# An index spread in two row tiles of TensorE, with the expert layer's issue order written anew

## The chip, the cores and the metric

The kernel runs on one core of one Trainium2 chip. The metric is the device time of one execution in microseconds (us). A core has five engines that work at the same time, each through its own list of instructions in order: TensorE (PE, matmuls; its weight loads are shown as PEld), VectorE (DVE), ScalarE (ACT), GpSimd (POOL) and SyncE (SP, which here issues the transfers). They wait for each other through semaphores. Matmul results land in PSUM, eight banks of 2 KB for each of 128 partitions, and have to be copied out by DVE or ACT.

## The reference

The input is 2048 tokens of 512 features. The first half is a state space convolution over the tokens (layer norm, an FFT convolution with a kernel made from 128 modes per feature, a skip). The second half is the expert layer, where the change lies:

```python
q1, q2 = q[..., :dk], q[..., dk:]          # q = layernorm(h) @ w_q, 32 heads
s1 = einsum("nhd,ed->nhe", q1, k1)         # 16 scores for each token and head
s2 = einsum("nhd,ed->nhe", q2, k2)         # 16 more
eidx = argmax(s1) * 16 + argmax(s2)        # K = 1: one of 256 experts
g = softmax over one score = 1
act = gelu(einsum("nd,nhd->nh", xf, u[eidx]))
out = einsum("nh,nhd->nd", act, v[eidx])   # sum over 32 heads
h2 = h + out
```

## The kernel before

The convolution is done as DFTs by matmul and takes most of the first 300 us. Behind it the expert layer goes through eight tiles of 256 tokens, b = 0 to 7. For each tile these steps run (the names are those of the tiles in the profile; a number behind a name is the tile b, or for mx, eq, kq, ks, ei and ix the half tile 2b + k of 128 tokens):

1. ib, h: the last step of the inverse transform on PE (L1036), with 32-column tiles of the array, and DVE's sum with the input xt (L1043).
2. hs, mean, hc, hhi, hlo: POOL adds four feature groups, PE sums over partitions, DVE subtracts the mean, ACT and DVE split the result into a high and a low part for exact products. vs, var, rstd do the same for the variance.
3. sc (L1150): scores for 960 columns, in four blocks per half tile, one for each quarter q of the features, each of which needs the weights w_hi and w_lo of that quarter. xu (L1157): products with all 256 rows of u; act: their gelu on ACT.
4. mx, eq, kq (DVE), ks (POOL), ei, ix (DVE): the place of the largest score, as a number from 0 to 255 for each token and head. ix is 128 tokens by 32 heads.
5. ixt, ixT: PE turns ix so that the 32 heads stand on 32 partitions (L1242), ACT copies it out (L1246).
6. bc, idxb: the index spread. For each g of 8, a matmul with the selection matrix sel_s[:, g] takes four heads and writes each on 32 partitions (L1258). Contraction is over the 32 partitions of ixT. Two matmuls of 256 tokens fill a PSUM bank, which ACT copies out as bf16 (L1262).
7. oh (L1280): DVE compares idxb with the expert codes, eight times per tile. cnt (L1290): PE counts the one-hots over the heads, with four 32-column tiles of the array. ta and actT bring act into the same layout; DVE multiplies.
8. whi, wlo, o, ob: the product with v in exact parts, the sum with h, and the store.

Tile 7 does steps 5 to 8 in two halves of 128 tokens, with all eight one-hots, counts and products for each half.

The code does not issue this in the order in which it is written. Each step is put in a list with `plan.add`, with its engine, what it reads and writes and which PSUM buffer it takes (`take="psD"`) or gives back. `plan.run(ORDER)` then issues the steps by a table of numbers. A number is the place of the step in the list of adds, so a step that is left out shifts all later numbers. An engine executes in that order and never passes a waiting instruction. The order also decides which buffers come next: psD has four buffers of a bank each, psC two of two banks for the scores. Transfers are all issued by SP, in order.

Before the expert layer the weights w_q0 to w_q3 are loaded, split by ACT (w_hi) and DVE (w_lo). They use the same buffers as later loads: w_q2 and w_q3 those of xt, and w_q0 and w_q1 those of sel_f (the selection matrix as loaded), u and v.

## Time and profile before

| | |
|---|---|
| time, median of 3 runs | 504.2 us (504.18 to 505.11) |
| profiled execution, its own time | 504.94 us |
| profiled execution, span from first to last instruction | 503.2 us |
| mean granted TensorE clock | 0.986 |
| PE busy | 449.0 us (89%) |
| DVE busy | 407.8 us (81%) |
| ACT, POOL busy | 298.3, 325.5 us |
| spread matmuls bc (L1258) | 56 of 256 columns, 16 of 128 |
| evictions idxb (L1262) | 32, 588 ns each, 17.5 us |

In rows of groups, the columns are: line, engine, operation, output<-input, partitions x elements, count | busy us, mean ns of one | idle time of the engine ahead of it and who ended that. The chain of waits has the start, the length and the piece. A timeline row has the start, the length, the engine, the line, the operation and, in brackets, the idle time ahead of it with its releaser. In the table of stretches each engine's busy us stands with its number of instructions, and then the clock, the share of DMA and GB/s. PE's busy time includes the pipelined tail of a matmul, so that of many short matmuls in a row is read from the starts or the chain, not from the mean.

### The profile page before, as it was taken

The numbers are of one execution on the slowest core, as the hardware profiler recorded it, in microseconds if no ns is written. First come the engines' busy times: TensorE is split into PE (matmuls) and PEld (weight loads), VectorE is DVE, ScalarE is ACT, GpSimd is POOL, SyncE is SP. The second block draws the span as 40 slices with busy tenths as digits, with TensorE's granted clock in tenths as the row PEclk, the third lists the DMA queues.
The fourth block names the chain that finished last, engine by engine and source line by source line (L and its number), as shares of the span: only waits on it lengthen the run. The fifth ranks groups of instructions, "written<-read, shape, count | busy, mean of one in ns | idle before, by whom it ended". The sixth has DMA issues, their size and how long they took to land.

```text
span 503.2 us, 16702 instructions
## 1 busy us (share of the span) xinstructions
PE 449.0 (89%) x7206; PEld 390.3 (78%) x7206; DVE 407.8 (81%) x708; ACT 298.3 (59%) x594; POOL 325.5 (65%) x344
## 2 busy tenths in 40 slices
PE   0266879999998999999998889999999999999985
PEld 0144568888997999889997787877878888787874
DVE  5998998899968998899745574888979686978984
ACT  4867799967987588967965362644043430416230
POOL 4989989999999999997824303572163516536130
PEclk9998799999999999999999899999999999999999
DMA  8959474234033300631017689310171311010012
GB/s 253 403 198 381 143 288 148 66 86 179 2 111 124 85 3 1 212 126 45 1 61 259 200 275 283 127 61 1 57 227 55 109 63 43 1 44 0 1 68 62
DMA packets 27362, 61.05 MB, mean 121 GB/s; under 512 B 7028, under 2 KB 14456, under 8 KB 26136
## 3 DMA queue, kind: packets, MB, share of 16 engines
q1 hardware_dynamic: 27136, 59.85, 34.9%
q8 instruction: 57, 0.93, 0.7%
q10 hardware_dynamic: 152, 0.13, 0.1%
q14 instruction: 17, 0.14, 0.1%
HBM read 46.08 MB, written 13.89 MB: 119 GB/s over the span
## 4 chain that ended last, share of the span: by engine, by line
PE 50%; DVE 22%; ACT 10%; POOL 10%; issue 4%; DMA 3%; SPq 1%; ACTq 0%; DVEq 0%; POOLq 0%
PE sc L1150 12%; PE ia L764 9%; DVE oh L1280 5%; PE s2yk L488 3%; PE xu L1157 3%; PE kps L690 3%; PE s2yu L488 3%; POOL pg L557 3%; PE s1u L471 3%; DVE st L232 2%; PE o L1327 2%; PE ib L1036 2%; PE cnt L1290 2%; ACT t L645 2%; POOL mg L594 2%
## 5 line engine op out<-in xcount | busy, mean ns | idle before, releaser
L557 POOL TENSOR_TENSOR pg<-PS 128x1024 int32<-128x1024 int32 x32 | 68.8, 2150 | 0.5
L588 POOL TENSOR_TENSOR mg<-TS 128x1024 f32<-128x1024 f32 x32 | 62.6, 1958 | 7.2 <-PE kps L690 4.5
L1280 DVE TENSOR_SCALAR oh<-idxb,ec_s 128x2048 bf16<-128x2048 bf16 (+1 forms) x72 | 50.3, 757 | 6.8 <-ACT idxb L1262 6.8
L764 PE MATMUL ia<-ca_s,U 128*128 128x128 f32 x256 | 50.6, 280 | 0.4 <-POOL U L743 0.4
L1060 POOL TENSOR_TENSOR vs<-hc 128x256 f32<-128x256 f32 x8 | 7.0, 872 | 62.6 <-ACT hc L1083 62.6
L1192 POOL TENSOR_TENSOR ks<-kq 128x512 f32<-128x512 bf16 x16 | 17.2, 1078 | 45.9 <-DVE kq L1186 44.8
L645 ACT ACTIVATE t<-t,halfpi 128x512 f32<-128x512 f32 x64 | 42.4, 662 | 2.1
L1150 PE MATMUL sc<-w_hi,hhi 128*128 128x480 f32 x128 | 42.4, 412 | 0.0
L644 ACT ACTIVATE t<-pg 128x512 f32<-128x512 int32 x64 | 38.9, 609 | 3.2 <-DVE gf L652 2.2
L764 PEld LDWEIGHTS ia<-ca_s,U 128*128 128x128 f32 x256 | 39.8, 196 | 0.6 <-POOL U L743 0.6
L647 ACT ACTIVATE t<-pg 128x512 f32<-128x512 int32 x64 | 38.2, 608 | 2.8 <-POOL pg L557 1.5
L764 PE MATMUL ia<-ca_s,yk 128*128 128x128 f32 x192 | 38.1, 280 | 0.4 <-DVE mg L664 0.4
L1150 PE MATMUL sc<-w_lo,hhi 128*128 128x480 f32 x128 | 38.4, 380 | 0.0
L1150 PE MATMUL sc<-w_hi,hlo 128*128 128x480 f32 x128 | 38.3, 380 | 0.0
L594 POOL TENSOR_TENSOR mg<-TS 128x512 f32<-128x512 f32 x32 | 37.4, 1170 | 0.4
L690 PE MATMUL kps<-mg 128*32 128x64 f32 x1024 | 34.0, 230 | 3.8 <-DVE mg L664 2.2
L488 PE MATMUL s2yk<-yk,c_s 128*128 128x128 f32 x256 | 34.7, 282 | 1.1 <-ACT yk L474 0.7
L471 PE MATMUL s1u<-c_s,xs 128*64 128x128 f32 x512 | 33.3, 277 | 2.5 <-DVE xs L508 1.6
L690 PE MATMUL kps<-gf 128*32 128x64 f32 x1024 | 33.7, 229 | 1.8 <-issue 1.8
L488 PEld LDWEIGHTS s2yk<-yk,c_s 128*128 128x128 f32 x256 | 30.6, 191 | 4.2 <-issue 1.4
L488 PE MATMUL s2yu<-yu,c_s 128*128 128x128 f32 x256 | 32.6, 279 | 0.3
L471 PEld LDWEIGHTS s1u<-c_s,xs 128*64 128x64 f32 x512 | 27.6, 137 | 5.4 <-DVE xs L508 1.7
(198 smaller groups left out, 1377.5 us busy)
## 6 DMA issues: line engine op xcount, KB each, us to landing
wq<-wq SPq DMA_DIRECT2D x25, 512.0 KB, 4.5
t_d<-T SPq DMA_DIRECT2D x24, 256.0 KB, 3.4
Tb<-t_d SPq DMA_DIRECT2D x8, 768.0 KB, 6.0
x<-xa SPq DMA_DIRECT2D x8, 512.0 KB, 5.6
xs<-xb SPq DMA_DIRECT2D x16, 256.0 KB, 5.3
xt<-xt SPq DMA_DIRECT2D x8, 512.0 KB, 4.8
out<-ob SPq DMA_DIRECT2D x7, 512.0 KB, 3.0
c_s<-wq SPq DMA_DIRECT2D x4, 512.0 KB, 8.3
```

The costliest lines, as they stand in the source:

```text
L471: T.matmul(ps[64 * k:64 * k + 64, g, :], lhs8(4 * n + g), c1_s[:, k], start=True, stop=True)
L488: T.matmul(ps[:, k, :], c2_s[:, kk, :], y[:, :, kk, :], start=True, stop=True)
L557: G.tensor_tensor(view(pg, 0, [[32, 2 * NC], [8, 4], [1, 8]]), view(t["PS"], 1024 + off, [[1, 2 * NC], [128, 4], [0, 8]]), view(t["PS"], 8 ...
L588: G.tensor_tensor(view(mg, 0, [[96, NC], [8, 8], [1, 8]]), view(ts, 512 + 8 * o, [[8, NC], [1, 8], [0, 8]]), view(ts, 8 * o, [[8, NC], [0, ...
L594: G.tensor_tensor(view(mg, 64, [[96, NC], [8, 4], [1, 8]]), view(ts, 1536 + o, [[1, NC], [64, 4], [0, 8]]), view(ts, 1024 + 8 * o, [[8, NC ...
L644: A.activation(p, pg[:, :, k], AF.Abs)
L645: A.activation(p, p, AF.Sin, scale=-SINSCALE, bias=halfpi)
L647: A.activation(p, pg[:, :, k], AF.Sin, scale=SINSCALE)
L690: T.matmul(kps[32 * q:32 * q + 32, 2 * g + h, :], m[:, d, 64:96], m[:, d, 0:64], start=(e == 0), stop=(e == 1))
L764: T.matmul(ps[:, g, :], t[:, 4 * n + g].rearrange("p a b -> p (a b)"), ca_s[:, s, :], start=(s == 0), stop=(s == 1))
L1150: T.matmul(ps[:, 512 * h:512 * h + 480], t[x_][:, q, ts], I[w_][:, q, 480 * h:480 * h + 480], start=(q == 0 and x_ == w_), stop=(q == 3 an ...
L1280: V.tensor_scalar(oh[:, :, 0:ln], t["idxb"][:, :, sl], S["ec"][:, 4 * e + j:4 * e + j + 1], None, op0=ALU.is_equal)
```

## The change

ix is written twice side by side, 64 columns instead of 32. The transpose then turns both copies at once, so that ixT has 64 partitions: heads 0 to 31 on partitions 0 to 31 and again on 32 to 63. The selection matrix is stored twice in the same way. The eight spread matmuls of a tile are issued in pairs: the first of a pair contracts over partitions 0 to 31, the second over 32 to 63, and the two write into two different PSUM buffers. One step of PE now takes two psD buffers and holds four matmuls (eight of 128 columns in tile 7); the evictions stay as they were, one for each buffer. There are 16 steps fewer in the list, 1712.

```diff
 def sel_load():
-    ...name="sel_f").rearrange("p a b -> p (a b)")[0:32].rearrange(
+    ...name="sel_f").rearrange("p a b -> p (a b)")[0:64].rearrange(
...
-        S["sel"] = I["wp"].tile([32, 8, 128], BF16, name="sel_s")
+        S["sel"] = I["wp"].tile([64, 8, 128], BF16, name="sel_s")
...
-            t[f"ix{k}"] = hp_("ix", n, [P, 32], BF16)
-            V.scalar_tensor_tensor(t[f"ix{k}"], ef[:, :, 0], 16.0, ef[:, :, 1], op0=ALU.mult, op1=ALU.add)
+            t[f"ix{k}"] = hp_("ix", n, [P, 64], BF16)
+            a, b_ = (ef[:, :, j].unsqueeze(1).to_broadcast([P, 2, 32]) for j in range(2))
+            V.scalar_tensor_tensor(t[f"ix{k}"].rearrange("p (c h) -> p c h", c=2), a, 16.0, b_, op0=ALU.mult, op1=ALU.add)
...
-                job["ps"] = tp = I["psD"].tile([32, 256], BF16, tag="m", name=f"ixt{b}_{lo}")
+                job["ps"] = tp = I["psD"].tile([64, 256], BF16, tag="m", name=f"ixt{b}_{lo}")
...
-            for g in range(0, 8, hj):
+            for g in range(0, 8, 2 * hj):
...
-                    job["ps"] = bp = I["psD"].tile([P, hj, ln], F32, tag="m", name=f"bc{b}_{g}_{ln}")
+                    for r in range(2):
+                        job[r] = I["psD"].tile([P, hj, ln], F32, tag="m", name=f"bc{b}_{g}_{ln}_{r}")
                     for h in range(hj):
-                        T.matmul(bp[:, h], S["sel"][:, g + h, :], t["ixT"][:, sl], start=True, stop=True)
+                        for r in range(2):
+                            rs = slice(32 * r, 32 * r + 32)
+                            T.matmul(job[r][:, h], S["sel"][rs, g + hj * r + h, :], t["ixT"][rs, sl], start=True, stop=True)
...
-                n = plan.add("PE", 0.23, mm, r=[("ixT", p), "sel"], t=[kX, kB], take="psD", n_mm=hj)
-                plan.add("ACT", 0.50, ev, w=[("idxb", p, g)], t=[kB], give="psD", after=[n])
+                n = plan.add("PE", 0.27, mm, r=[("ixT", p), "sel"], t=[kX, kB], take=("psD", "psD"), n_mm=2 * hj)
+                for r in range(2):
+                    ...
+                    plan.add("ACT", 0.50, ev, w=[("idxb", p, g + hj * r)], t=[kB], give="psD", after=[n])
...
 ORDER:
-    954, 1090, 955, 1091, 1092, 956, 1094, 957, 958, 1099, 1104, 1118, 1119, 1206, 1120, 1095, 1096, 1097, 1100, 1101,
+    954, 1090, 955, 1091, 1092, 956, 1094, 957, 958, 1099, 1104, 1118, 1119, 1120, 1095, 1096, 1097, 1100, 1101, 1102,
...
```

The table is the same up to the steps with which the convolution ends, and another one behind them. What that moves is shown at three places. A number at the end of a name only tells buffers apart, and so do the line numbers, which are one less in the changed kernel up to the change and some more behind it.

First, PE in tile 0's spread (bc0), with its transposes ixt0 and the scores sc1_1 ahead of it. Before:

```order
L1150 MATMUL sc1_1_4786<-w_hi_4192,hlo1_4644 128x480 x2
L1258 LDWEIGHTS sel_s_4359
L1258 MATMUL bc0_4_256_4835<-ixT0_4833,sel_s_4359 128x256
L1258 LDWEIGHTS sel_s_4359
L1258 MATMUL bc0_4_256_4835<-ixT0_4833,sel_s_4359 128x256
L1258 LDWEIGHTS sel_s_4359
L1258 MATMUL bc0_2_256_4838<-ixT0_4833,sel_s_4359 128x256
```

and changed:

```order
L1149 MATMUL sc1_1_4734<-w_hi_4192,hlo1_4615 128x480 x2
L1261 LDWEIGHTS sel_s_4356
L1261 MATMUL bc0_0_256_0_4851<-ixT0_4832,sel_s_4356 128x256
L1261 LDWEIGHTS sel_s_4356
L1261 MATMUL bc0_0_256_1_4852<-ixT0_4832,sel_s_4356 128x256
L1261 LDWEIGHTS sel_s_4356
L1261 MATMUL bc0_0_256_0_4851<-ixT0_4832,sel_s_4356 128x256
```

Two matmuls in a row used to fill one buffer (bc0_4); now they alternate between the two buffers of a pair, each with its own rows of sel_s and ixT.

Second, DVE where the expert layer starts. Before:

```order
L925 TENSOR_TENSOR w_lo_4193<-w_q1_4309,w_hi_4192 128x960
L925 TENSOR_TENSOR w_lo_4193<-w_q0_4312,w_hi_4192 128x960
L1043 TENSOR_TENSOR h0_4418<-ib0_0_4366,xt0_4316 128x4x128
L1043 TENSOR_TENSOR h0_4418<-ib0_1_4383,xt0_4316 128x4x128
L1073 TENSOR_TENSOR hc0_4463<-h0_4418,mean0_0_4458 128x4x128
L1073 TENSOR_TENSOR hc0_4463<-h0_4418,mean0_1_4467 128x4x128
L1080 TENSOR_TENSOR hlo0_4527<-hc0_4463,hhi0_4465 128x4x128
L1043 TENSOR_TENSOR h1_4530<-ib1_1_4441,xt1_4331 128x4x128
L1080 TENSOR_TENSOR hlo0_4527<-hc0_4463,hhi0_4465 128x4x128
```

and changed:

```order
L924 TENSOR_TENSOR w_lo_4193<-w_q0_4300,w_hi_4192 128x960
L1042 TENSOR_TENSOR h0_4414<-ib0_1_4363,xt0_4345 128x4x128
L1042 TENSOR_TENSOR h0_4414<-ib0_0_4381,xt0_4345 128x4x128
L1072 TENSOR_TENSOR hc0_4455<-h0_4414,mean0_1_4450 128x4x128
L1072 TENSOR_TENSOR hc0_4455<-h0_4414,mean0_0_4457 128x4x128
L1079 TENSOR_TENSOR hlo0_4465<-hc0_4455,hhi0_4463 128x4x128
L977 CAST sel_s_4356<-sel_f_4503 64x1024
L1079 TENSOR_TENSOR hlo0_4465<-hc0_4455,hhi0_4463 128x4x128
L924 TENSOR_TENSOR w_lo_4193<-w_q1_4501,w_hi_4192 128x960
```

The w_lo of w_q1 moved from ahead of h0 to behind hlo0, and the cast of the selection matrix in between the halves of hlo0. On SP the load of w_q1 accordingly moved behind those of xt1 and xt0, and xt3 ahead of u and v.

Third, DVE at the start of the last three tiles (ix13 is the last index of tile 6; oh40 to oh47 are tile 5's, oh48 to oh55 tile 6's; mx14 is the largest score of tile 7's first half). Before:

```order
L1202 SCALAR_TENSOR_TENSOR ix13_6657<-ei13_6655 128x32
L1280 TENSOR_SCALAR oh44_6675<-idxb5_6620,ec_s_4198 128x2048
L1280 TENSOR_SCALAR oh42_6677<-idxb5_6620,ec_s_4198 128x2048
L1280 TENSOR_SCALAR oh43_6679<-idxb5_6620,ec_s_4198 128x2048
L1280 TENSOR_SCALAR oh41_6681<-idxb5_6620,ec_s_4198 128x2048
L1280 TENSOR_SCALAR oh40_6689<-idxb5_6620,ec_s_4198 128x2048
L1280 TENSOR_SCALAR oh45_6725<-idxb5_6620,ec_s_4198 128x2048
L1280 TENSOR_SCALAR oh47_6727<-idxb5_6620,ec_s_4198 128x2048
L1280 TENSOR_SCALAR oh46_6729<-idxb5_6620,ec_s_4198 128x2048
L1280 TENSOR_SCALAR oh51_6811<-idxb6_6717,ec_s_4198 128x2048
L1280 TENSOR_SCALAR oh49_6813<-idxb6_6717,ec_s_4198 128x2048
```

and changed:

```order
L1202 SCALAR_TENSOR_TENSOR ix13_6690<-ei13_6688 128x64
L1284 TENSOR_SCALAR oh45_6701<-idxb5_6637,ec_s_4198 128x2048
L1284 TENSOR_SCALAR oh43_6703<-idxb5_6637,ec_s_4198 128x2048
L1284 TENSOR_SCALAR oh47_6705<-idxb5_6637,ec_s_4198 128x2048
L1284 TENSOR_SCALAR oh44_6707<-idxb5_6637,ec_s_4198 128x2048
L1284 TENSOR_SCALAR oh42_6733<-idxb5_6637,ec_s_4198 128x2048
L1284 TENSOR_SCALAR oh41_6735<-idxb5_6637,ec_s_4198 128x2048
L1284 TENSOR_SCALAR oh40_6744<-idxb5_6637,ec_s_4198 128x2048
L1284 TENSOR_SCALAR oh46_6786<-idxb5_6637,ec_s_4198 128x2048
L1175 TENSOR_REDUCE mx14_6831<-sc7_0_6676 128x64
L1284 TENSOR_SCALAR oh50_6833<-idxb6_6724,ec_s_4198 128x2048
```

mx14 stands behind eight one-hots now, where before fifteen and a product stood ahead of it. Everything else in DVE's list from here to the end is the same work in nearly the same order. On PE at the same place, mean7 (the mean of tile 7) stands ahead of tile 5's spread and behind both xu5, where before one xu5 and four matmuls of that spread stood ahead of it. At the very end all eight spread matmuls of tile 7's second half stand ahead of the first half's counts (cnt7_0); before, four of them stood between the two parts of these counts.

12 lines of the change are left out of this document (6 added, 6 removed), and 67 rows, old and new, of the table ORDER.

## The prediction

> **What bounds the kernel now.** I read the page's totals first, then the table of stretches over the expert layer, then the chain of waits, then the groups of the spread, and last the timelines of the few places where the chain changes engine.
>
> ```profile
> span 503.2 us, 16702 instructions
> PE 449.0 (89%) x7206; PEld 390.3 (78%) x7206; DVE 407.8 (81%) x708; ACT 298.3 (59%) x594; POOL 325.5 (65%) x344
> ...
> core 0: us, PE busy (x) PEld busy (x) DVE busy (x) ACT busy (x) POOL busy (x), PEclk, DMA share, GB/s
> 350.00:370.00 20.00, 19.56 (x320) 17.47 (x312) 19.34 (x27) 2.00 (x5) 6.62 (x10) 1.00 0.21 69
> 390.00:410.00 20.00, 20.00 (x266) 17.22 (x266) 15.10 (x24) 8.41 (x15) 7.32 (x11) 1.00 0.32 107
> 470.00:490.00 20.00, 18.56 (x184) 16.62 (x182) 18.76 (x32) 6.58 (x12) 5.82 (x8) 1.00 0.08 31
> ```
>
> The diff leaves the first 282 us alone, so only the expert layer matters. In it TensorE (PE) is full in the middle (20.00 of 20 us at 390 to 410), while VectorE (DVE) is nearly full twice: at 350 to 370 (19.34) and at 470 to 490 (18.76). PE work that is removed counts only in the middle stretches.
>
> ```profile
> 335.45 0.54 PE bc L1258 x4
> 345.81 1.50 PE sc L1150 x6
> 347.32 0.76 PE bc L1258 x6
> 348.07 0.99 PE cnt L1290 x32
> 349.06 0.32 PE bc L1258 x2
> ...
> L1258 PE MATMUL bc<-ixT,sel_s 32*128 32x256 bf16 x56 | 8.7, 270 | 0.0
> L1262 ACT CAST idxb<-bc 128x512 bf16<-128x512 f32 x32 | 17.5, 588 | 11.3 <-PE bc L1258 11.3
> L1202 DVE SCALAR_TENSOR_TENSOR ix<-ei 128x32 bf16<-128x32 int32 x16 | 6.1, 381 | 0.6
> ```
>
> The first five lines are pieces of the chain (start, length): spreads (bc) of two, four and six matmuls take 0.32, 0.54 and 0.76 us. Each matmul costs 0.11 and each group another 0.10. The mean of 270 ns in the group line is latency, not throughput. The spread of one tile of 256 tokens therefore costs PE 8 x 0.11 = 0.88 us and two group costs.
>
> **The change, part by part.** *The spread itself.* Eight matmuls per tile stay eight, but they go in pairs to rows 0 to 31 and rows 32 to 63, each of a pair into its own PSUM bank. No row here shows two row tiles side by side. The bounds: a pair takes 0.22 as now (no overlap), or 0.11 (full overlap); and above, a change of row tile could cost the group's 0.10 each time, 0.21 per matmul. The nearest row is cnt: 32 matmuls of the same 256 columns, which go to four column tiles in turn, take 0.99 us, 0.031 each against 0.11 for a spread alone. I take full overlap: 0.44 saved per tile.
>
> The Trainium skill, "TensorE: Matmul & The Clock Gate" (Part 3, measured speedup), gives 3.07 times for four row tiles of K=32, less than full overlap. Taken in proportion for two tiles that is an estimate of 1.54 times: 0.88 becomes 0.57, 0.31 saved per tile, and the sum below would end 0.5 us later. No run here shows it yet.
>
> *Its costs.* The index is written twice (64 columns for 32) 16 times. A DVE step this small is mostly fixed: between nothing and double its 381 ns mean, nearer to nothing since uncontended ones take 0.19 us (below); 0.03 us each, 0.5 in all, of which four or five lie where DVE is full: 0.1. The transposes stream the same 128 columns; evictions keep their free size (64 partitions for 32), so nothing on ACT. sel doubles to 256 KB; a load of u, twice as large, lands in 7.6 us (below), which bounds it.
>
> *The start of the expert layer.* This is order, not spread.
>
> ```profile
> 299.51 2.23 DVE w_lo L925 x2
> 301.77 0.70 DVE h L1043
> 302.52 2.05 PE mean L1093 x16
> 304.57 1.46 PE ib L1036 x90
> 307.10 4.12 PE sc L1150 x18
> ...
> 307.76 0.67 DVE L978 CAST sel_s<-sel_f 32x1024 bf16<-32x1024 f32 x1
> ...
> 293.67 2.30 SPq L1014 DMA_DIRECT2D xt<-xt  x2
> 303.51 0.40 SPq L975 DMA_DIRECT2D u_raw<-ue  x1
> ...
> u_raw<-ue SPq DMA_DIRECT2D x1, 512.0 KB, 7.6
> ```
>
> Two w_lo (2.23 us) stand on the chain ahead of the first h; the new order keeps one there (w_q0), the other comes after hlo0. That takes up to 1.1 us off; PE's own ib for tile 0 must be done as well, so I take 0.9: scores at 306.2. The moved w_lo (1.1) is needed only for the second quarter of the scores, and ahead of it run two blocks of 1.5: hidden; without that cover its 1.1 comes back. The same holds for the sel cast (0.67), now between the halves of hlo0: it delays the second half, not the first block. On SP's queue the load of w_q1 is moved past Tb1 and both xt, which wait for slots until 293.67 to about 296. All of these bytes are the same as before and xt1 was the last of them, so w_q1 should land by about 301, 7 us ahead of its use.
>
> SP also now has xt3 ahead of u and v, and xt3 waits for h1. I put h1 at 308.5, so u is issued near 309, not 303.51, and lands near 317 at 7.6; v behind it. On ACT the v_hi cast stands ahead of rstd0 and u_hi, and waits with them. By the new order u_lo is needed after all of tile 0's scores and six of tile 1's eight blocks, near 328.5. Slack: about 5 us after the casts of v and u. Hidden.
>
> *What of the 0.9 lives on.* DVE's full stretch begins at its first one-hot:
>
> ```profile
> 332.54 0.19 DVE L1202 SCALAR_TENSOR_TENSOR ix<-ei 128x32 bf16<-128x32 int32 x1
> ...
> 340.75 1.02 DVE L1202 SCALAR_TENSOR_TENSOR ix<-ei 128x32 bf16<-128x32 int32 x1
> 341.69 0.15 DVE L1134 RECIPROCAL rstd<-rstd 128x2 f32<-128x2 f32 x1
> 341.77 3.40 DVE L1280 TENSOR_SCALAR oh<-idxb,ec_s 128x2048 bf16<-128x2048 bf16 x4
> ```
>
> In the new order the first one-hot stands ahead of ei2, ix2 and rstd2 instead of behind, and PE reaches the second spread pair of tile 0 earlier. Walking the new rows with these durations I get its start at about 340.6, 1.2 earlier, but 0.5 us of small steps is then still to do. Lead into the DVE-full stretch: 0.6.
>
> *The middle.* From about 370 PE is the bound and the spreads of tiles 2 to 5 save 4 x 0.44 = 1.7. Ahead of ib7 lie three of them (1.3), but the new order also puts the last block of tile 6's scores (1.3 without a mode change) ahead of ib7: lead at ib7 0.6.
>
> ```profile
> 451.62 1.29 DVE L1043 TENSOR_TENSOR h<-ib,xt 128x512 f32<-128x512 f32 x2 [0.77 <-PE ib L1036]
> 454.61 0.74 POOL L1062 TENSOR_TENSOR hs<-hs,h 128x256 f32<-128x256 f32 x1
> 455.99 0.70 PE L1105 MATMUL mean<-hs,ones_d 128*128 128x256 f32 x2
> 456.73 1.22 DVE L1073 TENSOR_TENSOR hc<-h,mean 128x1024 f32<-128x1024 f32 x1
> 459.12 1.33 DVE L1080 TENSOR_TENSOR hlo<-hc,hhi 128x1024 fp32r<-128x1024 f32 x1 [1.18 <-ACT hhi L1076]
> 460.48 0.69 PE L1150 MATMUL sc<-w_hi,hhi 128*128 128x480 f32 x2
> ```
>
> From here a serial chain goes through all engines: h7, hs on POOL, mean7, hc7, hlo7, then sc7. hs ends at 455.35, and mean7 starts 0.64 later, since PE was in four spread matmuls ahead of it. In the new order tile 5's whole spread comes behind mean7, and PE, done with both xu5, will wait for POOL instead: 0.6 gained. Lead at hlo7 and the last DVE stretch: 0.6 + 0.6 = 1.2.
>
> *The end.*
>
> ```profile
> 460.73 10.13 DVE L1280 TENSOR_SCALAR oh<-idxb,ec_s 128x2048 bf16<-128x2048 bf16 x13
> 488.89 0.87 DVE L1280 TENSOR_SCALAR oh<-idxb,ec_s 128x1024 bf16<-128x1024 bf16 x2
> 492.13 0.42 DVE L1299 TENSOR_TENSOR actT<-cnt,actT 128x256 f32<-128x256 f32 x1 [2.37 <-PE ta L1227]
> 492.47 3.25 DVE L1280 TENSOR_SCALAR oh<-idxb,ec_s 128x1024 bf16<-128x1024 bf16 x8
> ...
> 496.97 2.05 PE L1324 MATMUL o<-actT,v_raw 128*128 128x128 f32 x16 [0.59 <-DVE actT L1299]
> 499.06 0.69 DVE L1332 TENSOR_TENSOR ob<-o,h 128x512 f32<-128x512 f32 x1 [1.55 <-PE o L1324]
> ```
>
> From 460.73 to 489.76 DVE runs the same list in both kernels, nearly without a gap, so the lead of 1.2 passes through. Then it waits 2.37, because PE does xu7_1, two spreads and two counts in between. The new order has all eight spread matmuls of the last half ahead of these counts, and only the second half of the counts waits for the last one-hot. From that one-hot (D): counts D+0.6, actT 1.1, eight one-hots 4.4, last counts 5.0, actT 5.5, o 7.5, ob 8.2, against 499.75 - 489.76 = 9.99 now. I take 1.5 of these 1.8, for the eviction of the last spread comes just in time.
>
> Sum: 1.2 + 1.5 - 0.1 = 2.6 us, so a span of 500.6. The profiled execution took 504.94, 1.7 over its span and 0.7 over the median of the runs (504.2; they go from 504.18 to 505.11). Against the median: 501.6.
>
> **Rivals.** *No overlap.* The row pairs run one after the other. The middle's 1.3 ahead of ib7 go, and 0.4 of tile 0's two pairs ahead of the first one-hot: 2.6 - 1.7 = 0.9 left, 503.3, on the line between faster and no change. For it: no row here shows two row tiles. Against it: cnt's 0.031 each over column tiles. The Trainium skill, "TensorEngine Tiling (Array Packing)" (Key Properties), says that different tiles run matmuls in parallel; no run here shows it for rows.
>
> *DVE waits for the last scores.* The new DVE list has mx14 after eight one-hots of tile 5 (8 x 10.13/13 = 6.2 us), where it had thirteen and more ahead. PE must finish four blocks of 1.5, a transpose and two spread groups in that time, about 6.9, so 0.7 is lost even as forecast runs; I have counted on it being made up at the next gap. If mx15 waits also, 2 us are lost: 503.6, no measurable change. Against it: PE gains on DVE after that. The Trainium skill, "TensorEngine Tiling (Array Packing)" (PSUM Bottleneck), speaks against the change: the copies out of PSUM may become the bound once tiling speeds TensorE up. Four evictions of 588 ns are 2.4 us per tile against under 0.9 of spread; if they set the first one-hot of each tile, the time is this rival's 503.6. The trace agrees so far that DVE waits for them (6.8 us for idxb over the layer):
>
> ```profile
> DVE oh L1280 <- ACT idxb L1262: 6.8, 3, 2.6
> ```
>
> *Every change of row tile drains.* If going from rows 0-31 to rows 32-63 costs what entering a spread costs (0.10), each group of four takes 4 x 0.21 = 0.84, 0.30 more than now. Tiles 2 to 4 lose 6 x 0.30 = 1.8 where 1.3 was won, and tile 0 loses 0.6 where 0.4 was won ahead of the first one-hot: 501.6 + 4.1 = 505.7, slower. It passes 505.2 from about 0.09 per change on. Against it: cnt changes column tile at each of 32 matmuls and pays nothing. The Trainium skill, "TensorEngine Tiling (Array Packing)" (Key Properties), says that a change of mode drains the array, and not a change of tile alone. The group cost of 0.10 agrees with the first half; no run here shows the second for rows.
>
> *u and v late.* If v lands after about 322.5 (13 us from issue; 7.6 is the row), xu0 stalls, and every microsecond goes to the end: from 326 on the time is over 505.2. Against it: the row above is little more than half of that.
>
> **How the numbers follow.** No change means within 0.2%, 1.0 us, about what a measurement can tell. Forecast 0.54, own range 500.2 to 503.0; no overlap 0.12 (half faster, half same); DVE waiting for scores, or another new wait of that size, 0.13 (same); draining 0.12 and late loads, or a longer stall in the new order, 0.09 (slower). Faster 0.60, same 0.19, slower 0.21. The range from 499.8 (0.3 more at the end, 0.6 more if all of the first one-hot's 1.2 is kept, and 0.9 if most of the 1.3 block ahead of ib7 falls into time that PE would have waited) to 505.6 leaves out one in ten on each side.
>
> **What would show it.** Right: a spread of four in 0.33 us in the chain (0.54: no overlap; over 0.8: drain); first scores near 306.2; first one-hot near 340.6; mean7 right behind hs; the last wait of DVE near 1 us. Wrong: PE waiting on evictions at a spread, DVE waiting on sc in the last tile, xu0 behind u_lo, or an ACT queue held by v_hi.

## The result and the profile after

The changed kernel is slower: 510.4 us median (509.9 to 514.8, 4 runs) against 504.2 for the one before, a ratio of 1.0133 with a 95% interval of 1.0092 to 1.0174. The forecast was 501.6, with a range up to 505.6. Timed again it was 1.0120 (1.0076 to 1.0163). Times of one kernel here spread over several us: 127 runs of the kernel before go from 502.1 to 509.0. A part of that goes with TensorE's clock, which falls to half in stretches that differ between runs (last section): runs with a mean granted clock of 0.99 or more took 504.0 on the mean, those with 0.98 or less 505.6. So profiles are compared below by stages without such a stretch.

The first lines are the page's totals of the changed kernel, the next its table of stretches (columns as in the first such table above). The last line is the stretch from 330 to 350 of the kernel before.

```profile
span 508.6 us, 16689 instructions
PE 451.3 (89%) x7206; PEld 390.4 (77%) x7206; DVE 414.1 (81%) x708; ACT 297.3 (58%) x594; POOL 329.4 (65%) x344
...
330.00:350.00 20.00, 17.00 (x108) 13.86 (x107) 17.14 (x24) 8.73 (x17) 14.27 (x17) 1.00 0.02 8
350.00:370.00 20.00, 20.00 (x352) 17.23 (x351) 18.09 (x27) 7.17 (x12) 3.98 (x6) 1.00 0.17 58
390.00:410.00 20.00, 20.00 (x265) 16.77 (x265) 14.91 (x21) 5.97 (x10) 9.77 (x14) 1.00 0.26 74
470.00:490.00 20.00, 19.01 (x220) 14.97 (x219) 19.91 (x28) 6.13 (x13) 6.74 (x8) 1.00 0.07 28
...
330.00:350.00 20.00, 20.00 (x151) 15.87 (x153) 16.16 (x23) 10.75 (x20) 10.92 (x14) 1.00 0.01 2
```

DVE is busy 6.3 us longer than before though it does the same operations (ix alone is wider). And there is a new hole: at 330 to 350 PE works 17.00 of 20 us, where it was full before, while POOL works 14.27 (10.92 before). The chain of waits of the changed kernel, in pieces:

```profile
308.89 8.05 PE sc L1149 x36
...
331.37 1.35 DVE u_lo L983
332.76 3.01 PE xu L1156 x23
...
339.43 0.32 PE bc L1261 x4
...
342.69 0.34 PE bc L1261 x4
...
344.16 1.90 DVE oh L1284 x2
...
462.29 0.64 PE mean L1104 x2
...
467.40 6.18 DVE oh L1284 x7
...
504.38 0.69 DVE ob L1336
```

The spread does what the diff says: four matmuls in 0.32 to 0.34 us, where they took 0.54. All the same the first scores come at 308.8 (before 307.0), the first one-hot at 344.16 (341.77), the first one-hot of the last full DVE stretch at 467.40 (460.73), and the last ob starts at 504.38 (499.06). Below, "the layer" is the time from the first score matmul to the end of the last ob: 192.72 us before, 196.25 after. Of the 5.3 us of the profile, 1.8 are lost ahead of the layer and 3.5 in it.

The groups of waits of PE in the layer of the changed kernel (total, times, longest) name what was not there before, when ixt<-ix was 0.4 and xu<-u_lo did not occur:

```profile
PE ixt L1242 <- DVE ix L1202: 2.1, 2, 1.6
PE cnt L1294 <- DVE oh L1284: 2.0, 6, 0.5
PE xu L1156 <- DVE u_lo L983: 1.4, 1, 1.4
PE xu L1156 <- DVE ob L1336: 1.0, 1, 1.0
```

(cnt<-oh was 1.2 before and xu<-ob 0.4.)

### The profile page after: what moved, and what is told of

Same layout as the page of the kernel before. It is cut to its first block, busy times and chain, and to the rows that moved or that the text cites. A ratio compares the mean times of both kernels' runs of the same rounds, so it can differ in the third digit from the quotient of the medians.

```text
span 508.6 us, 16689 instructions
## 1 busy us (share of the span) xinstructions
PE 451.3 (89%) x7206; PEld 390.4 (77%) x7206; DVE 414.1 (81%) x708; ACT 297.3 (58%) x594; POOL 329.4 (65%) x344
## 4 chain that ended last, share of the span: by engine, by line
PE 48%; DVE 25%; ACT 11%; POOL 9%; issue 4%; DMA 2%; SPq 0%; DVEq 0%; POOLq 0%; ACTq 0%
PE sc L1149 10%; PE ia L763 9%; DVE oh L1284 7%; PE kps L689 3%; PE s2yk L487 3%; PE xu L1156 3%; POOL pg L556 3%; PE s1k L470 3%; PE s1u L470 2%; PE ib L1035 2%; PE cnt L1294 2%; PE o L1331 2%; DVE st L231 2%; PE s2yu L487 2%; ACT idxb L1267 2%
## 5 line engine op out<-in xcount | busy, mean ns | idle before, releaser
L1284 DVE TENSOR_SCALAR oh<-idxb,ec_s 128x2048 bf16<-128x2048 bf16 (+1 forms) x72 | 53.0, 790 | 5.7 <-ACT idxb L1267 5.7
L689 PE MATMUL kps<-mg 128*32 128x64 f32 x1024 | 34.7, 233 | 3.1 <-DVE mg L663 1.4
L1193 POOL TENSOR_TENSOR ks<-ks 128x256 f32<-128x256 f32 (+2 forms) x48 | 31.6, 658 | 3.8
```

The costliest lines, as they stand in the source:

```text
L689: T.matmul(kps[32 * q:32 * q + 32, 2 * g + h, :], m[:, d, 64:96], m[:, d, 0:64], start=(e == 0), stop=(e == 1))
L1284: V.tensor_scalar(oh[:, :, 0:ln], t["idxb"][:, :, sl], S["ec"][:, 4 * e + j:4 * e + j + 1], None, op0=ALU.is_equal)
```

## The experiments

Ratios are to the kernel before, run on the same chip, with 95% intervals. Theories were: the spread itself loses (no overlap); the start loses; u_lo's wait in the front of the layer loses; the middle loses what the spread saves; GpSimd slows VectorE.

**Row tiles.** The changed kernel with both matmuls of a pair on the same rows:

```diff
-                            rs = slice(32 * r, 32 * r + 32)
+                            rs = slice(0, 32)
```

> The changed kernel in its order, with both matmuls of each pair reading rows 0-31 (no second row tile; the same banks, sizes and order). Theory A: a spread of four goes back to about 0.54 us; 16 groups of four (8 us of spread work) lose 0.21 each, 3.4 in all, of which 1.5 to 2.5 reach the end: 512.0 to 513.0 against 510.4. Theory B: no loss, 510.4 or less. Beside it, the first 300 us are the changed kernel's word for word: if its stretch of half clock at 274.3 to 277.7 belongs to that code and not to one execution, it shows here again.

Ratio 1.0116 (1.0081 to 1.0152). The chain of this kernel has the group of four back at its old price:

```profile
340.29 0.54 PE bc L1261 x4
```

The spread's busy time on PE in the layer was 10.1 us before, 9.5 here and 6.1 in the changed kernel. So the two row tiles overlap; by the chain's pieces a group of four saves 0.21 us, and sixteen such groups 3.4. In time this kernel could not be told from the changed kernel, which repeated gave 1.0120. In the stages it can: from the first one-hot to the end of the last ob it takes 161.95 us at full clock against 160.91 in the changed kernel, so the overlap is worth 1.0 us there, of 3.4 us of PE time. The repeated kernel:

> The changed kernel itself again, beside the others, as their measure: 196.0 to 196.5 us from the first scores to the last instruction, first scores at 308.2 to 308.9 whether or not a stretch of half clock falls into the time ahead of them, and a ratio to the kernel before of 1.008 to 1.013. A ratio under 1.006 would say that the first comparison had an unlucky share of half clock.

**The spread in the old order.** The order of before, renumbered, each merged pair where its first half stood:

```diff
-    954, 1090, 955, ... 1118, 1119, 1120, 1095, 1096, ...
+    954, 1090, 955, ... 1118, 1119, 1204, 1120, 1095, ...
```

> The order of the kernel before, kept step by step, with the new spread (two copies of the indices, row tiles 0-31 and 32-63, two PSUM banks taken at once; a pair of spread steps stands where its first one stood). Theory A (the new order and a lost stretch of clock cost the time, the spread itself gains): a spread of four takes 0.33 us in the chain as in the changed kernel, TensorE (PE) spends 4.0 us less on spreads (10.1 to 6.1), of which 1 to 2 lie where PE is the bound; 502.2 to 503.5 against 504.2. Theory B (taking two banks at once, or the evictions, eat what the overlap gives): 504.2 or above, with PE or VectorE waiting at the spreads; 505.5 and more if the spread is the cause of the loss.

Ratio 1.0038 (1.0007 to 1.0068): no gain, rather a loss. PE's busy time in the layer fell from 187.52 to 184.87 us, but the layer grew from 192.72 to 193.94: PE's idle time rose from 5.2 to 9.1 us. The waits of PE in this kernel, and below them the place of the longer of the two waits for h (PE and DVE timelines):

```profile
PE cnt L1294 <- DVE oh L1284: 3.0, 3, 1.7
...
PE bc L1261 <- DVE h L1042: 1.0, 2, 0.6
...
370.99 0.28 PE L1261 MATMUL bc<-ixT,sel_s 32*128 32x256 bf16 x1
371.90 0.37 PE L1261 MATMUL bc<-ixT,sel_s 32*128 32x256 bf16 x3 [0.63 <-DVE h L1042]
...
371.15 1.29 DVE L1042 TENSOR_TENSOR h<-ib,xt 128x512 f32<-128x512 f32 x2 [0.55 <-PE ib L1035]
```

The pair's first matmul goes to one free bank; its second needs another, which holds an ib until DVE has evicted h. A step that took one bank of four now takes two at once, and waits for the later. The Trainium skill, "TensorEngine Tiling (Array Packing)" (PSUM Bottleneck), says that copies out of PSUM may become the bottleneck once tiling speeds TensorE up. This trace agrees for 1.0 us of PE's waits: they end when DVE has read ib out of its bank.

Moving the spreads of tiles 2 and 3 behind one more score block, out of the way of h:

```diff
-    ... 1421, 1324, 1325, 1273, 1375, 1321, 1322, 1360, 1364, 1326,
+    ... 1421, 1273, 1375, 1324, 1325, 1360, 1364, 1321, 1322, 1326,
...
-    ... 1391, 1392, 1395, 1397, 1492, 1393, 1495, 1496, 1446, 1386,
+    ... 1391, 1492, 1495, 1496, 1446, 1392, 1393, 1395, 1397, 1386,
```

> The order of the kernel before with the new spread, and the four spread steps of tiles 2 and 3 one block of scores later (behind the eviction of the h halves, which hold two of the four small PSUM banks). Theory B2 (a pair needs two banks at once and waits for the eviction of h by VectorE; that wait of about 0.9 per tile eats the 0.44 it saves): the waits of the spread at 371 and 397 (0.63 and 0.38 us) go, the stretch from xu of tile 2 to the end of ib of tile 6, 53.15 us without the shift and 52.18 in the kernel before, falls to 51.3 to 51.8, and the layer takes 192.0 to 193.0 instead of 193.9. Rival: the wait only moves, 193.5 or more.

Ratio 1.0052 (1.0027 to 1.0077): no gain. The wait for h is gone and another stands in its place, for the evictions (waits of PE in this kernel):

```profile
PE var L1123 <- ACT idxb L1267: 0.8, 1, 0.8
...
PE ta L1227 <- ACT idxb L1267: 0.5, 1, 0.5
```

Spreading tiles 2 and 3 as before, in four groups of two, the rest in pairs:

```diff
+            for g in range(0, 8, hj) if b in (2, 3) else ():
...
+                        T.matmul(bp[:, h], S["sel"][0:32, g + h, :], t["ixT"][0:32, sl], start=True, stop=True)
...
+            for g in () if b in (2, 3) else range(0, 8, 2 * hj):
```

> The order of the kernel before with the new spread, but tiles 2 and 3 spread as before, in four groups of two matmuls from rows 0-31, each with one PSUM bank. Theory B2 (only where h and the pair need banks at once does the pair lose): PE's waits for h at the spread (1.0 in all) go, the stretch from xu of tile 2 to the end of ib of tile 6 takes 52.2 again instead of 53.15, the layer 192.7 to 193.2, ratio 0.999 to 1.003. Rival: the layer stays at 193.7 or more, then the loss in the old order lies in other tiles.

Ratio 1.0026 (1.0000 to 1.0052). No wait of bc for h is left in it, but cnt<-oh keeps its 3.0 us. Between 1.0038 and 1.0026 the measured times do not decide. The stage does, and no half clock falls into it in these profiles: from the start of tile 1's first ob to the first one-hot of the last full DVE stretch there are 92.95 us before, 94.02 with all tiles in pairs, 93.96 with the pairs of tiles 2 and 3 later, and 93.39 here. So pairs cost 1.1 us in the middle of the old order, and 0.6 of it is due to those of tiles 2 and 3. In the old order, then, the spread buys nothing.

**The start.** The old order up to the first score step, then the new one (from the unchanged line on), run twice:

```diff
-    954, 1090, 955, ... 1118, 1119, 1120, 1095, 1096, ...
+    954, 1090, 955, ... 1118, 1119, 1204, 1120, 1095, ...
...
     ... 1280, 1215, 1216, 1157, 1277, 1148, ...
```

> The order of the kernel before up to the first score step of tile 0 (loads, w_hi, w_lo, the evictions of T, all as before, on all engines), then the new order for what is left; new spread. Theory E (the new start costs: the first w_hi stands on ScalarE behind two T evictions instead of four, waits there for its load, and holds up the other T evictions, ib0 and h0): the first scores come at 304.9 at full clock, as in the old order with the new spread, against 308.24 in the new order at full clock, and the whole gains 2.5 to 3.3: ratio to the kernel before about 1.002 to 1.005 where the new order with u_lo early has 1.008. Rival F (the start is paid back later, since the layer is bound elsewhere): the ratio stays at 1.007 to 1.010.

> The kernel with the old start and the new order behind it, a second time, since its one profile (first scores at 306.05) and its timed runs (as slow as those with the new start) did not agree. Theory E: first scores again 1.2 to 3.3 us earlier than 308.2, ratio 1.003 to 1.007. Rival F: the ratio stays within 0.002 of that of the changed kernel, so the start is not where the time went.

Ratios 1.0085 (1.0054 to 1.0116) and 1.0066 (1.0043 to 1.0090), layers of 196.50 and 196.53: the layer is as slow as in the changed kernel, and by the medians 0.35 to 0.7% come back, with intervals that overlap those of the changed kernel. Over all profiles of the study the first scores come at 308.2 on the mean with the new start (eight, 306.5 to 308.9) and at 306.8 with the old one (ten, 304.8 to 308.6). So the start loses about 1.5 us on the mean, where I forecast a gain of 0.9. ACT's timeline of the changed kernel, then of the one before, shows a wait that was not there:

```profile
289.61 0.74 ACT L776 COPY T<-ia 64x256 f32<-64x256 f32 x2 [1.33 <-PE ia L763]
292.86 0.99 ACT L923 CAST w_hi<-w_q 128x960 fp32r<-128x960 f32 x1 [2.51 <-DMA w_q<-w_d]
293.76 1.50 ACT L776 COPY T<-ia 64x256 f32<-64x256 f32 x4
...
290.69 0.74 ACT L777 COPY T<-ia 64x256 f32<-64x256 f32 x2 [1.04 <-PE ia L764]
291.46 0.99 ACT L924 CAST w_hi<-w_q 128x960 fp32r<-128x960 f32 x1
```

The new order has the first cast of w_hi behind two of ACT's evictions of T instead of four. There ACT waits 2.51 us for the load of w_q, with the other evictions queued behind it, and tile 0's ib needs those. The wait is 1.9 to 5.3 us in all nine profiles with the new start (the eight above and the one with extra matmuls below), and at most 0.03 in seven of the ten with the old one (1.0, 1.2 and 3.2 in the others). In six of the nine the chain of waits ahead of the first scores goes through this load. In the profile shown it does not: there PE's ia matmuls run without a gap from 284.3 to 300.3, at half clock up to 288.0 (before: from 283.8 to 297.8, at half clock up to 285.4), so a part of its 1.8 us is the clock's. No run moved the casts of w_hi alone: that the start's order as a whole loses is shown, that this wait is the reason is likely.

A rival explanation was TensorE's clock. Extra matmuls keep PE busy in its waits there:

```diff
+                for _ in range(6 if (c, n) == (3, 0) else 0):
+                    T.matmul(ps[:, 0, :], ident, ident, start=True, stop=True)
...
+            for _ in range(14 if n == 28 else 4 if n > 28 else 0):
+                T.matmul(j1["o"], ident, ident, start=True, stop=True)
```

> The changed kernel with 42 extra matmuls of 128x128 (0.11 us each, their results are overwritten) that fill PE's waits ahead of the expert layer: 14 in the wait for the load of wq at 271.7 to 273.6, the others before the next transposes and the first inverse matmul, 278 to 284. Theory C (PE's idle time ahead of the layer makes the clock fall to half, at 274.3 to 277.7 and 284.5 to 287.9): both stretches show a granted clock of 1.00, the first scores start 2.5 to 3.5 us earlier than 308.89, and 506.9 to 507.9 comes out. Rival D (the loads or VectorE's products set the pace there): scores stay near 308.9, 510.4; if the extra work only adds up, 512 to 514.

Ratio 1.0173 (1.0144 to 1.0203). The clock stayed at 1.00 from 270 to 291, and still the first scores came at 312.3: with the extra matmuls (80 by the page, not 42) the store of w_d was issued at 286.7 instead of 283.6, and w_hi waited 5.3 us for its load instead of 2.5. Work that looks free held up a transfer. But a stretch of half clock came at 305.8 instead, so this run does not settle the rival. Three profiles without any half clock from 60 us to the first scores do: these come at 308.2 with the new start (one, the kernel with u_lo early below) and at 304.8 and 306.1 with the old one (the old order with the new spread, and the same with less GpSimd below). The start loses without the clock too.

**The front of the layer.** u_lo ahead of tile 0's second index on DVE:

```diff
-    ... 1170, 1171, 1150, 1223, 1127, 1125, 1233, ...
+    ... 1170, 1125, 1171, 1150, 1223, 1127, 1233, ...
```

> The changed kernel with one step moved: u_lo on VectorE ahead of the second index of tile 0 instead of behind it, rstd0 and v_lo. Theory A1 (the new order's late u_lo stalls PE and this reaches the end): the wait of the first xu (1.44 us from 331.3 to 332.8) goes, all later stages start 1.0 to 1.4 earlier, 509.0 to 509.4. Rival A2 (VectorE's later stages set the pace, so the stall was covered): the wait goes but the first one-hot moves less than 0.5 and the time stays within 0.2% of 510.4.

Ratio 1.0079 (1.0049 to 1.0109), but the layer takes 196.07 us: the 1.4 us wait is gone and only 0.2 came of it. Its successor in PE's timeline of this kernel:

```profile
334.71 0.70 PE L1104 MATMUL mean<-hs,ones_d 128*128 128x256 f32 x2 [1.27 <-POOL hs L1061]
```

With hs2 earlier on GpSimd too, and tile 1's indices ahead of the first one-hots:

```diff
-    ... 1155, 1159, 1160, 1172, 1283, 1229, ...
+    ... 1155, 1283, 1159, 1160, 1172, 1229, ...
...
-    1226, 1294, 1190, 1185, 1231, 1186, 1241, 1242, ...
+    1226, 1294, 1231, 1190, 1185, 1241, 1242, 1186, ...
```

> The changed kernel with local moves in the first 60 us of the layer: u_lo ahead of the second index of tile 0 on VectorE, hs of tile 2 one step earlier on GpSimd, and the two indices of tile 1 ahead of the first and second one-hot instead of the third and fourth. Theory G: PE's waits at 331 to 333 (1.4) and 347.6 to 349.2 (1.6) go, and 1.5 to 2.9 of them reach the end: layer 193.3 to 194.7. Rival H: the waits move to the next place, 195.5 to 196.2.

Ratio 1.0088 (1.0058 to 1.0119), layer 196.12: the waits moved once more (a bc now waits 1.1 for ixT). Here a stall of PE that was removed alone only moved the wait to the next step. Putting the whole old front back, up to the second xu step of tile 2 at about 366 us, with the new order from the unchanged line on:

```diff
-    954, 1090, 955, ... 1118, 1119, 1120, 1095, 1096, ...
+    954, 1090, 955, ... 1118, 1119, 1204, 1120, 1095, ...
...
     ... 1560, 1559, 1339, 1370, 1371, 1431, ...
```

> The order of the kernel before up to the second xu step of tile 2 (about 366 us), then the new order for the rest; new spread. Theory G (in the first 60 us of the layer the new order loses another 2.5 to 2.9 us, by u_lo, hs2 and the indices of tile 1 that come late; behind it, it is as good as the old one): from the first scores to the last instruction 192.3 to 193.5 us, against 196.2 in the changed kernel, ratio to before 0.999 to 1.003. Rival H (the later part of the new order loses as well, or what the front lost was work done ahead for later): 194.5 to 196 us for the layer, ratio 1.005 and more.

Ratio 1.0035 (1.0009 to 1.0061), layer 194.16. Against the old start alone the front is worth 2.3 us. Behind it the steps take as long as in the changed kernel, to within 0.1 us.

**GpSimd.** In the front of the changed kernel DVE and POOL run like this (timelines of DVE, PE and POOL):

```profile
346.92 0.74 DVE L1284 TENSOR_SCALAR oh<-idxb,ec_s 128x2048 bf16<-128x2048 bf16 x1
347.59 0.74 DVE L1198 TENSOR_SCALAR ei<-ks 128x64 int32<-128x64 int32 x1
348.36 0.77 DVE L1202 SCALAR_TENSOR_TENSOR ix<-ei 128x64 bf16<-128x64 int32 x1
...
349.18 0.24 PE L1242 MATMUL ixt<-ident_b,ix 128*64 128x128 bf16 x1 [1.56 <-DVE ix L1202]
...
347.00 1.25 POOL L1060 TENSOR_TENSOR vs<-vs,hc 128x256 f32<-128x256 f32 x1
348.32 0.72 POOL L1061 TENSOR_TENSOR vs<-vs,hc 128x256 f32<-128x256 f32 x1
```

ei and ix take 0.74 and 0.77 us, and each ends 0.08 to 0.09 after the POOL addition beside it (348.25 and 349.04). That addition in turn takes 1.25 beside a one-hot. Two of the three additions of each variance sum were then left out (half of the features stay in the sum, not a quarter, as one of the expectations below has it):

```diff
-            G.tensor_tensor(s_, s_, q[:, 2], op=ALU.add)
-            G.tensor_tensor(s_, s_, q[:, 3], op=ALU.add)
+            for j in (2, 3) if src == "h" else ():
+                G.tensor_tensor(s_, s_, q[:, j], op=ALU.add)
```

> The changed kernel without two of the three additions in each sum of squares (vs) on GpSimd: the variance is then that of half the columns; 16 additions of 0.74 us are gone, 11.8 us of GpSimd's work. Theory I (in the new order VectorE's 16-bit steps run beside busy GpSimd more often, 1.03 us for a one-hot against 0.67 alone, and this makes the VectorE-full front longer): the one-hots' mean falls from 790 to 730-760 ns, VectorE's busy time by 2 to 4 us, the layer to 194.0 to 195.3. Rival J (the front is set by the order of its waits): VectorE's busy time falls but the layer stays at 195.8 to 196.5.

Ratio 1.0032 (1.0007 to 1.0058), from 1.012. I took this for the cause, until the control was run, with the changed kernel once more and the old order with the new spread beside it; the edit is the same in all:

> The kernel before, without two of the three additions of each variance sum on GpSimd (8 x 2 additions, 13 us of GpSimd; the variance then covers a quarter of the features). It is the control for the changed kernel with the same left out. Theory (the new order runs GpSimd's additions beside VectorE's small steps and one-hots where VectorE or PE wait for them, and this is what it loses in the layer): before loses little by GpSimd, so this gains under 0.2%, ratio 0.998 to 1.000, layer 192.0 to 192.7 us, and the changed kernel keeps its own gain of 0.9%. Rival (GpSimd costs both orders alike): ratio 0.990 to 0.993, and GpSimd explains nothing of the difference between the orders.

> The changed kernel with the same two additions of each variance sum left out, once more, beside its control on one chip. Both theories: ratio to before 1.001 to 1.005 (1.0032 the first time), layer 193.0 to 193.5 us when no half clock falls in it; the index of tile 1's second half takes 0.2 us instead of 0.77. What decides is its distance to the old order with the same left out: Theory: 0.3 to 0.6% above it, the late start alone (1.8 us). Rival: 1.0 to 1.3% above it, as the two whole kernels stand to each other.

> The order of before with the new spread in it, and the same two additions left out. The loss of this kernel was put down to pairs that wait for two PSUM banks and to evictions, not to GpSimd. Theory: no gain over the same kernel with all additions beyond what the order of before gains, ratio 1.002 to 1.005. Rival (GpSimd delays the halves of h that hold the banks): ratio 0.994 to 1.000.

Ratios 0.9965 (0.9944 to 0.9985), 1.0044 (1.0015 to 1.0072) and 0.9981 (0.9962 to 1.0000). The old order gains too, 0.35%. The new order stays 0.8% above it, between the two forecasts (0.3 to 0.6, and 1.0 to 1.3). In the old order with the new spread GpSimd also has a larger part than I thought. At the place shown above, now with POOL idle (DVE and PE timelines of the changed kernel without the additions):

```profile
346.48 0.20 DVE L1198 TENSOR_SCALAR ei<-ks 128x64 int32<-128x64 int32 x1
346.71 0.23 DVE L1202 SCALAR_TENSOR_TENSOR ix<-ei 128x64 bf16<-128x64 int32 x1
...
346.99 0.24 PE L1242 MATMUL ixt<-ident_b,ix 128*64 128x128 bf16 x1 [0.47 <-DVE ix L1202]
```

Two more runs without the additions divide what remains. The first also has u_lo early, as above; the second has the old front:

> The changed kernel without two of the three additions of each variance sum on GpSimd, and with u_lo ahead of the second index of tile 0, as was tried alone. Against the changed kernel with the additions alone left out (layer 193.14 us, ratio 1.0044). Theory (in the front of the layer PE waits for a chain of small steps, and the wait for u_lo gave no gain alone because the next wait, for hs2 on GpSimd, took its place): with less GpSimd work the 1.3 us wait is a gain, layer 191.8 to 192.3, ratio 1.001 to 1.003. Rival (the front is set by DVE's list, whatever PE waits for): layer 192.9 to 193.3, ratio 1.004 to 1.005.

> The order of before up to the second xu step of tile 2 and the new order behind it (layer 194.16 us, ratio 1.0035 with all additions), without two of the three additions of each variance sum. The order of before with the same left out has a layer of 191.49 us and ratio 0.9965. Theory (behind the front the new order with the new spread is as good as the old one once GpSimd is out of the way; what remains of the changed kernel's loss lies in its start and front): layer 191.0 to 191.7, ratio 0.995 to 0.998. Rival (the new order loses behind the front too): layer over 192.2, ratio 1.000 or more.

Ratios 1.0034 (1.0004 to 1.0063) and 0.9981 (0.9959 to 1.0004). The layers of the five orders, from profiles without a stretch of half clock in the layer:

| order, spread | all additions | two of three left out | difference |
|---|---|---|---|
| old, as before | 192.72 | 191.49 | 1.23 |
| old, new spread | 193.94 | 192.10 | 1.84 |
| old front, new behind, new spread | 194.16 | 191.87 | 2.29 |
| new, new spread | 196.25 | 193.14 | 3.11 |
| new with u_lo early, new spread | 196.07 | 193.06 | 3.01 |

Each is one profile; layers of nearly the same order (196.07 and 196.25 with 196.12, 196.50 and 196.53) differ by up to 0.5. Of the 3.53 us by which the layer grew, 3.11 - 1.23 = 1.9 go through GpSimd, 193.14 - 191.87 = 1.3 are the front, and 191.87 - 191.49 = 0.4 are left. Whether the 1.9 come from slower DVE steps or from GpSimd's own shorter queue was not separated; DVE's busy time in the layer falls by 4.1 us in the new order (161.0 to 156.9) and by 1.8 in the old (153.7 to 151.9).

The same profiles by stage (in the changed kernel the layer starts at 308.82 and the stages end at 344.16, 372.45, 467.40 and 505.07) show that the 0.4 is the balance of a loss and a gain:

| order, spread | to the first one-hot | to tile 1's first ob | to the last full DVE stretch | to the end |
|---|---|---|---|---|
| old, as before | 34.74 | 26.01 | 92.95 | 39.02 |
| old, new spread | 34.82 | 26.22 | 94.02 | 38.87 |
| old front, new behind, new spread | 35.24 | 26.23 | 94.95 | 37.74 |
| new, new spread | 35.34 | 28.29 | 94.95 | 37.67 |
| old, as before, two left out | 34.41 | 26.01 | 92.85 | 38.22 |
| new, new spread, two left out | 35.22 | 27.17 | 94.01 | 36.74 |

The third column repeats to within 0.07 in the eight profiles that run the changed kernel's steps there. The changed kernel loses 2.3 us up to tile 1's first ob and 2.0 in the middle, where the spread itself loses 1.1 in the old order, and gains 1.3 at the end. Leaving out the additions takes nothing off the old order up to that ob and 1.1 off the new one. u_lo's wait is not the 1.3, nor a gain without the additions (0.08): again PE waits for the next thing (its waits in that kernel):

```profile
PE mean L1104 <- POOL hs L1061: 1.2, 1, 1.2
```

Which of the front's waits makes the 1.3 stays open, and so does what the new order loses in the middle beyond the spread's 1.1. Of the kernels that do the whole work, none beat the one before; the nearest was 1.0026.

## Why the prediction was wrong

- *The spread.* Right: 0.33 us for a group of four, full overlap; "no overlap" and "draining" are out. I took 8 x 0.44 = 3.5 of PE time for all tiles; 16 groups of four at 0.21 less make 3.4. What was wrong is what became of it (see the middle).
- *ix twice.* Right in size: uncontended ix took 0.19 and takes 0.23.
- *The start (scores at 306.2, 0.9 early).* Wrong in sign: 308.8 in the first profile and 1.5 us late on the mean. I followed the w_lo that left DVE's list, and checked the load of w_q1; I did not check where the first w_hi stands in ACT's queue against its load. The wait there, 1.9 to 5.3 us, was in no term.
- *u and v (slack of 5 us).* Wrong: u was issued at 311.7 instead of 309, and u_lo then stood behind ei0, rstd0 and v_lo on DVE until 331.3, not 328.5. I sized the loads and not the queue behind them: the chain goes from POOL's ks through ei and ix, which took 1.03 and 0.78 us there beside POOL, to v_lo and u_lo. But the 1.4 us that PE waited were not the loss: two experiments took them away for at most 0.2.
- *The first one-hot (340.6; lead 0.6).* It came at 344.16, of which 1.8 is the late start; the order itself lost 0.6 (35.3 us after the first score against 34.7). From there to tile 1's ob the old order needs 26.0 us and the new 28.3. This step failed most in price: I walked the new rows with the durations of the old ones, 0.2 for a small step, and beside POOL they took 0.7. A duration was a property of the neighbour; the prediction's own rows had an ix of 1.02 us at 340.75 beside the one of 0.19. Of the 2.3 us between these two marks 1.1 go through GpSimd: they are gone with the additions left out, which take nothing off the old order there.
- *The middle (1.7 saved by the spreads).* Wrong. It did not come: from tile 1's first ob to the last full DVE stretch the changed kernel takes 2.0 us longer (94.95 against 92.95). With the old order the saving is there in PE's busy time and absent from the clock: over the layer PE worked 2.65 us less and waited 3.9 more, for DVE's one-hots and for the second PSUM bank of a pair. In this stage PE was idle for 0.9 us before, 2.5 in the old order with the new spread and 2.3 in the changed kernel. I had put "PE is the bound" for the whole stretch at 370 to 460. The new order also has PE busy 1.1 us longer there than the old one with the same spread (92.6 against 91.5 us); why stays open.
- *mean7 behind hs.* Right as an order (hs ends 462.16, the matmul starts 462.22), without a lead to pass on: from tile 1's first ob to the last, both orders take 131 to 132 us, the middle's loss and the end's gain together.
- *The end (1.5).* Right: from the first one-hot of the last stretch to the last ob 38.3 us before and 37.0 after, 1.3 gained. DVE's wait ahead of actT there fell from 2.37 to 0.98, as forecast (near 1 us):

```profile
497.43 0.43 DVE L1303 TENSOR_TENSOR actT<-cnt,actT 128x256 f32<-128x256 f32 x1 [0.98 <-ACT idxb L1267]
```

- *The rivals.* "DVE waits for evictions" named a part of what happened in the old order with the new spread (oh<-idxb 7.4 there, 6.8 before); for the last scores DVE did not wait at all, mx14 and mx15 start without a gap at 474.15 and 484.50. "A longer stall in the new order" had 0.09 together with late loads; a late start had nothing, and it cost 1.5 us.

So of the 2.6 us forecast the 1.3 at the end came and the middle's gain turned into waits. The profile is 5.3 longer with these 1.3 in it: 6.6 were lost, 1.8 at the start, 2.9 from there to tile 1's first ob and 2.0 in the middle. The step that failed is the claim that the moved steps are hidden and cost what they cost before, with a lead of 0.9 from the start and 0.6 from the first one-hot; the runs showed a late start, small steps slowed beside GpSimd, and pairs that wait for banks.

## What to carry to other kernels

A written order is a set of slacks on every queue: before trusting that a moved step is hidden, look at what stands behind the first instruction on each engine that waits for a transfer, and price steps moved beside GpSimd by rows where GpSimd runs. Work removed from the busiest engine counts only as far as the next engine and the buffers follow; a step that takes two of four buffers at once can wait longer than it saves. An experiment that leaves work out of the changed kernel needs the same left out of the old one: here 1.2 of the 3.1 us that it gained were not the change's.

## What was not expected of the hardware

*VectorE beside GpSimd.* Operations on bf16 and int32 in SBUF slow down: ei 0.20 to 0.74 us and ix 0.23 to 0.77, as shown. The one-hot (128x2048 bf16), from its start to the next instruction's, takes 0.66 us with POOL idle and 0.66 to 1.46, 1.00 at the median, with POOL busy over 80% of it; the changed kernel has 17 such among 56, the one before 12. mx and eq, which read f32 scores from PSUM, stay at 1.15 us either way. Over the layer the one-hots' group shows it, in the changed kernel with all additions and with two of three left out, and in the kernel before with all and with two of three left out:

```profile
L1284 DVE TENSOR_SCALAR oh<-idxb,ec_s 128x2048 bf16<-128x2048 bf16 (+1 forms) x72 | 53.0, 790 | 5.7 <-ACT idxb L1267 5.7
...
L1284 DVE TENSOR_SCALAR oh<-idxb,ec_s 128x2048 bf16<-128x2048 bf16 (+1 forms) x72 | 50.8, 760 | 5.7 <-ACT idxb L1267 5.7
...
L1280 DVE TENSOR_SCALAR oh<-idxb,ec_s 128x2048 bf16<-128x2048 bf16 (+1 forms) x72 | 50.3, 757 | 6.8 <-ACT idxb L1262 6.8
...
L1280 DVE TENSOR_SCALAR oh<-idxb,ec_s 128x2048 bf16<-128x2048 bf16 (+1 forms) x72 | 48.9, 737 | 7.0 <-ACT idxb L1262 6.9
```

The Trainium skill, "SBUF — State Buffer" (Who interferes with whom), has the rule that I should have weighed: VectorE and GpSimd share one pair of ports, and who holds it keeps it for the whole instruction. The trace agrees: ei and ix end right behind the POOL additions.

*The clock.* TensorE's granted clock fell to half for stretches of 3.41 us on a fixed grid, behind grid windows in which PE had worked little. Stretches of the changed kernel:

```profile
270.84:274.25 3.41, 1.56 (x26) 1.21 (x24) 3.25 (x6) 1.17 (x2) 3.05 (x3) 1.00 0.67 269
274.25:277.66 3.41, 3.41 (x26) 2.66 (x27) 1.95 (x4) 0.85 (x2) 1.70 (x3) 0.51 0.54 154
...
281.08:284.49 3.41, 1.88 (x37) 1.23 (x28) 3.28 (x7) 1.65 (x6) 2.84 (x3) 1.00 0.00 0
284.49:287.90 3.41, 3.41 (x17) 3.41 (x18) 0.18 (x2) 0.36 (x1) 0.00 (x0) 0.51 0.84 231
```

After 1.56 and 1.88 us of PE work in a window the clock halved for the next. Half a window did not always do it: the grid window from 345.99 had 1.85 us of PE work, and the clock stayed at 1.00 behind it. Over the 19 profiles, from 60 us on and without the last window, the clock halved behind all eight windows with PE busy 46% or less and behind none with 63% or more; between these both happened. The same kernel run again had its half clock at 302 to 306 and 333 to 336.5, so where it falls varies from run to run. The Trainium skill, "TensorE: Matmul & The Clock Gate" (Part 1), gives the window as 3413 ns, free-running; the grid agrees. It speaks of idle windows; here windows that were half busy sufficed.
